# A fused 2-D Fourier transform and two-layer MLP on one core: x in six tiles of 128 partitions, the weights' sign decoded on ScalarE, four plain steps, and the order of all pieces written anew

## The chip, the core and the metric

One core of a Trainium2 chip runs the whole kernel. The metric is the device time of one execution in microseconds (us); three runs of the kernel before gave a median of 1582.02 us. Engines are named as in the profile: PE is TensorE's matmul, PEld its weight load, DVE is VectorE, ACT is ScalarE, POOL is GpSimd, SP is SyncE, which issues the DMAs.

## What is computed

```python
def reference(x, moe_w_in, moe_w_out, moe_s, moe_b):
    # x: 8 x 3008 x 256, float32
    X = np.fft.fft(x, axis=1)
    X = np.fft.fft(X, axis=2)
    t = X.real.astype(np.float32).reshape(8 * 3008, 256)
    h = t @ moe_w_in                       # 256 x 2048
    r = np.maximum(h, 0.0)
    g = moe_s * (r * r) + moe_b
    return (g @ moe_w_out).astype(np.float32)   # 2048 x 256
```

## The kernel before

The eight batches of x are called `su` = 0 to 7. For each, x is read in tiles of 96 partitions by 1024 numbers (`load`, eight tiles for a batch), folded by sums and differences into `cs`, and turned by small matmuls with tables `dft_sb` into the spectrum (`transform`, twice a batch: `ph` 0 and 1, four `pair` calls of eight small matmuls each). The Nyquist column is done apart for all batches at once (`nyquist`). The transform along the features is not made at all: it is folded into `w_in` by matmuls with a table `feat_sb` (`fold_w_in`, four pieces f = 0 to 3).

The weights arrive as words of 64 bits. `decode` turns one piece of 128 x 512 words into float32: two passes on ACT, two operations on DVE (one shifts, one puts the sign in) and one add on POOL. Sixteen pieces are decoded, eight of `w_in` and eight of `w_out`.

After that comes the long part: 8 batches x 3 blocks of 502 columns x 16 slices of the hidden layer are 384 steps. In a step `first_layer` (letter L) makes six matmuls of 502 columns, three per kind, from the spectrum's high and low part and `w_in`'s; DVE forms `even` and the two halves of `h`, ACT takes relu, square and a rounded copy `gh`, POOL or DVE the rest `gl`. `second_layer` (letter S) makes twelve matmuls of 502 columns. The first PLAIN steps are different: ACT takes relu and square alone, and the second layer has four float32 matmuls (eight records in the profile) straight from the decoded `w_out`, before that is split into a high and a low part.

Work is issued in the order of a list written by hand: `START` and, for each further batch, `BATCH` are strings of letters, and each letter runs the next piece of one generator (l: load a piece of the next batch's x, v and o: its transforms, L, G, S: first layer, the low part, second layer; X, x, y: load and fold batch 0; r, a, b, e: load and decode weights; w: fold a piece of `w_in`; n, m: Nyquist; s, u: the transforms of batch 0). `_in_order` then keeps each engine in that order. Six tiles of x, the raw words and several working tiles share buffers, so a load waits until the tile before it was read.

Of the kernel before, what the change touches and what calls it, by code (L numbers as in the profile page):

```python
# [15 lines left out]
P = 128  # L16
# [4 lines left out]
R = 96  # L21
# [6 lines left out]
ENGINES = tuple(getattr(mybir.EngineType, e) for e in ("PE", "DVE", "Activation", "Pool"))  # L28
# [11 lines left out]
Y_ON_VECTOR = (0, 1, 2, 5)  # L40
X_ON_VECTOR = (0, 1, 2, 3, 5, 6, 7)
LOADS_ON_GPSIMD = ()
SUMS_ON_SCALAR = ()
PLAIN = 6
WORDS = (
    ("in", 0, 0), ("in", 0, 1), ("in", 1, 0), ("in", 1, 1), ("out", 0), ("out", 1), ("in", 2, 0), ("out", 2),
    ("in", 2, 1), ("out", 3), ("in", 3, 0), ("out", 4), ("in", 3, 1), ("out", 5), ("out", 6), ("out", 7),
)
START = (
# [7 lines left out]
)  # L57
BATCH = (
# [60 lines left out]
def _dft_tables():  # L119
# [3 lines left out]
    out = np.zeros((R, 2, 2, 8, NL), np.float64)  # L123
# [84 lines left out]
def _lay_out_x(x):  # L208
# [8 lines left out]
    xq = np.ascontiguousarray(padded[:, rows[..., None], order[swap]])  # L217
    xn = np.ascontiguousarray(padded[:, rows, P].transpose(1, 2, 3, 0))
# [18 lines left out]
def kernel(ctx: ExitStack, tc: tile.TileContext, xq, xn, dft, turn, feat, w_in, w_out, s, b, out):  # L237
# [10 lines left out]
    act = ctx.enter_context(tc.tile_pool(name="act", bufs=3))  # L248
    outp = ctx.enter_context(tc.tile_pool(name="outp", bufs=2))
# [16 lines left out]
    turn_sb = const.tile([R, 8], F32, name="turn_sb")  # L266
# [4 lines left out]
    wo_h = const.tile([P, NJ, D], F32R, name="wo_h")  # L271
    wo_l = const.tile([P, NJ, D], F32R, name="wo_l")

    def words(part):
        if part[0] == "out":
            f = part[1]
            return w_out[f * 256:(f + 1) * 256].rearrange("(j p) (d t) -> p j (d t)", p=P, t=2)
        _, f, c = part
        return w_in[c * P:(c + 1) * P, None, f * 1024:(f + 1) * 1024]

    def load_words(part, pool, tag):
        raw = pool.tile([P, 512, 2], I32, name="raw", tag=tag)
        src = words(part)
        nc.sync.dma_start(raw.rearrange("p (j d) t -> p j (d t)", j=src.shape[1]), src)
        return raw

    halves = {}
    wny_dram = dram.tile([1, FF], F32, name="wny_dram")

    def decode(part, raw, aux):  # L290

        low, high = raw[:, :, 0], raw[:, :, 1]
        bits = aux if len(aux.shape) == 2 else aux[:, 1]
# [11 lines left out]
        if part[0] == "in":  # L305
            halves[part[1:]] = w, aux[:, 0].bitcast(F32)
        yield
# [15 lines left out]
    def fold_w_in(f):  # L323

        (w0, row), (w1, _) = (halves[f, c] for c in range(2))
        row = row[0:1]
        at = slice(f * 512, (f + 1) * 512)
        for kind in range(2):
            ps = bank()
            for c, w in enumerate((w0, w1)):  # L330
                nc.tensor.matmul(ps, feat_sb[:, c, kind * P:(kind + 1) * P], w, start=c == 0, stop=c == 1)  # L331
            if f == 0 and kind == 1:

                column = ps_o.tile([P, 512], F32, name="po")
                for i in range(4):
                    for c, w in enumerate((w0, w1)):
                        nc.tensor.matmul(  # L337
                            column[:, i:i + 1], w[:, i * P:(i + 1) * P], feat_sb[:, c, P:P + 1],
                            start=c == 0, stop=c == 1,
                        )  # L340
            yield
            if kind == 1:
                if f == 0:
                    nc.scalar.copy(wny[:, :4], column[:, :4])
                else:
                    nc.scalar.copy(row, ps[0:1])
            split(wd_h[:, kind, at], wd_l[:, kind, at], ps, nc.vector)
        if f > 0:
            nc.sync.dma_start(wny_dram[:, at], row)
            nc.sync.dma_start(wny[:, 4 * f:4 * f + 4], wny_dram[0, at].rearrange("(j p) -> p j", p=P))  # L350
# [53 lines left out]
    def nyquist(ph, t, room):  # L404
# [3 lines left out]
        cs = t[:, :, 2 * ph + 1]  # L408
# [55 lines left out]
        e = room if ph else outp.tile([P, 2 * NT], F32, name="e", tag="o")  # L464
# [419 lines left out]
```

## Time and profile before

| | us |
|---|---|
| runs | 1581.05, 1582.02, 1583.15 |
| median | 1582.02 |
| span of the profiled execution, first to last instruction | 1580.4 |
| PE busy / PEld / DVE / ACT / POOL | 1557.5 / 1372.7 / 1208.8 / 1227.1 / 912.5 |

Busy time is the time in which an engine has an instruction at work; a wait is put down to what ended it. The span is one execution, and it lies 1.6 us under the median of the runs; what lies outside it is not in the profile. In timeline and chain lines the first number is the start in us from the span's start, the second the length in us.

### The profile page before, as it was taken

Reading aid. Unit: us, or ns where it says so; the run is one execution under the profiler, and the core shown is the slowest. Engines: PE = TensorE matmul, PEld = TensorE weight load, DVE = VectorE, ACT = ScalarE, POOL = GpSimd, SP = SyncE. Lnnn points to the kernel's source line nnn. Section 1 sums busy time; section 2 is a strip of 40 time slices with the busy share of each in tenths; the row PEclk is TensorE's granted clock in tenths of the full one; section 3 lists DMA queues with packets and bytes.
Section 4 is the critical chain, followed back from the end, with each engine's and each line's share of the span. In section 5 each row is a group of like instructions: output and inputs, shape, how many; then the busy total and the mean of one; then the engine's idle time right before and its main releaser. Section 6 shows DMA issues by size and latency. Waiting matters only on the chain.

```text
span 1580.4 us, 21929 instructions
## 1 busy us (share of the span) xinstructions
PE 1557.5 (99%) x7502; PEld 1372.7 (87%) x7502; DVE 1208.8 (76%) x1997; ACT 1227.1 (78%) x1305; POOL 912.5 (58%) x552
## 2 busy tenths in 40 slices
PE   5999999999999999999999999999999999999998
PEld 3688888888888888888988889888888888888887
DVE  7888788887868778687787878778787777865563
ACT  3889778877787787697877877778787778787886
POOL 4646556655565555565655656555566555665554
PEclk9999999999999999999999999999999999999999
DMA  7311211111002110121000210112101110000000
GB/s 209 98 57 57 63 31 34 47 57 43 8 28 72 31 44 7 37 64 46 27 33 21 63 37 27 34 30 64 53 1 34 47 47 34 8 27 33 1 26 27
DMA packets 25572, 67.41 MB, mean 43 GB/s; under 512 B 4915, under 2 KB 10259, under 8 KB 25462
## 3 DMA queue, kind: packets, MB, share of 16 engines
q1 hardware_dynamic: 25462, 66.01, 13.4%
q8 instruction: 60, 0.98, 0.3%
q14 instruction: 50, 0.41, 0.1%
HBM read 41.27 MB, written 24.73 MB: 42 GB/s over the span
## 4 chain that ended last, share of the span: by engine, by line
PE 98%; DMA 1%; DVE 0%; ACT 0%; SPq 0%; issue 0%; ACTq 0%; DVEq 0%
PE po L696 61%; PE ab L642 31%; PE ab L566 4%; PE po L687 1%; PE ab L331 1%; DMA dft_sb<-in_dft 1%; DMA xt<-in_xq 0%; PE ab L462 0%; DVE o L713 0%; PE po L337 0%; SPq L731 0%; ACT g L665 0%; ACT h L652 0%; ACTq L872 0%; DVE even L647 0%
## 5 line engine op out<-in xcount | busy, mean ns | idle before, releaser
L677 POOL TENSOR_TENSOR gl<-h,gh 128x1004 fp32r<-128x1004 f32 x372 | 803.1, 2160 | 562.9 <-ACT gh L674 402.8
L652 ACT ACTIVATE h<-h 128x1004 f32<-128x1004 f32 x384 | 398.4, 1037 | 169.6 <-DVE h L651 168.4
L674 ACT CAST gh<-h 128x1004 fp32r<-128x1004 f32 x378 | 389.0, 1029 | 123.2 <-PE po L696 113.1
L647 DVE SCALAR_TENSOR_TENSOR even<-ebc,wny,ab 128x502 f32<-128x502 f32 x384 | 281.9, 734 | 239.5 <-PE ab L642 230.9
L696 PE MATMUL po<-gh,wo_h 128*128 128x502 f32 (+1 forms) x1512 | 445.9, 376 | 0.1
L696 PE MATMUL po<-gh,wo_l 128*128 128x502 f32 (+1 forms) x1512 | 443.5, 375 | 0.0
L668 ACT ACTIVATE h<-h 128x1004 f32<-128x1004 f32 x378 | 393.5, 1041 | 12.0
L696 PE MATMUL po<-gl,wo_h 128*128 128x502 f32 (+1 forms) x1512 | 381.8, 375 | 0.0
L696 PEld LDWEIGHTS po<-gl,wo_h 128*128 128x128 f32 x1512 | 285.8, 189 | 34.3
L696 PEld LDWEIGHTS po<-gh,wo_l 128*128 128x128 f32 x1512 | 285.6, 189 | 34.4
L696 PEld LDWEIGHTS po<-gh,wo_h 128*128 128x128 f32 x1512 | 282.8, 189 | 34.2 <-DVE o L713 0.4
L650 DVE TENSOR_TENSOR h<-even,ab 128x502 f32<-128x502 f32 x384 | 260.2, 678 | 66.9 <-POOL gl L677 17.1
L642 PE MATMUL ab<-spec_h,wd_h 128*128 128x502 f32 x768 | 292.3, 381 | 0.0
L642 PE MATMUL ab<-spec_l,wd_h 128*128 128x502 f32 x768 | 288.3, 375 | 0.0
L642 PE MATMUL ab<-spec_h,wd_l 128*128 128x502 f32 x768 | 287.1, 374 | 0.0
L651 DVE TENSOR_TENSOR h<-even,ab 128x502 f32<-128x502 f32 x384 | 257.7, 671 | 0.0
L642 PEld LDWEIGHTS ab<-spec_h,wd_h 128*128 128x128 f32 x768 | 144.6, 188 | 19.9 <-issue 1.0
L642 PEld LDWEIGHTS ab<-spec_l,wd_h 128*128 128x128 f32 x768 | 144.7, 188 | 18.1 <-issue 1.2
L642 PEld LDWEIGHTS ab<-spec_h,wd_l 128*128 128x128 f32 x768 | 145.0, 189 | 17.5
L713 DVE TENSOR_SCALAR o<-po,sb_s,bias 128x502 f32<-128x502 f32 x94 | 68.8, 794 | 37.3 <-PE po L696 37.3
L554 POOL TENSOR_TENSOR spec_l<-o,spec_h 128x368 fp32r<-128x368 f32 (+3 forms) x80 | 62.8, 805 | 50.0 <-ACT spec_h L552 49.3
L497 DVE TENSOR_TENSOR xt<-xt 96x512 f32<-96x512 f32 x56 | 56.4, 1007 | 0.0
(99 smaller groups left out, 707.0 us busy)
## 6 DMA issues: line engine op xcount, KB each, us to landing
xt<-in_xq SPq DMA_DIRECT2D x64, 384.0 KB
out<-o SPq DMA_DIRECT2D x46, 502.0 KB
raw<-in_w_in SPq DMA_DIRECT2D x8, 512.0 KB
raw<-in_w_out SPq DMA_DIRECT2D x8, 512.0 KB
ebc<-e_dram SPq DMA_DIRECT2D x16, 251.0 KB
ebc<-e_dram SPq DMA_DIRECT2D x8, 126.0 KB
out<-o SPq DMA_DIRECT2D x4, 251.0 KB
ebc<-e_dram SPq DMA_DIRECT2D x8, 125.0 KB
```

The source lines that it names most:

```text
L554: nc.gpsimd.tensor_sub(lo, src, hi.bitcast(F32))
L566: nc.tensor.matmul(ps[:, kind, i], src[:, i, kind * P:(kind + 1) * P], dft_sb[:, ph, kind, leaf + i], start=True, stop=True,)
L642: nc.tensor.matmul(beside(ps[kind]), w[:, kind, fj], in_turn(m[:, kind]), start=i == 0, stop=i == 2)
L647: nc.vector.scalar_tensor_tensor(beside(even), in_turn(ebc), wny[:, j:j + 1], beside(ps[0]), op0=ALU.mult, op1=ALU.add)
L650: sub(h[:, 1], even, ps[1])
L651: add(h[:, 0], even, ps[1])
L652: nc.scalar.activation(h, h, AF.Relu)
L668: nc.scalar.activation(h, h, AF.Square)
L674: nc.scalar.copy(gh_halves, h)
L677: engine.tensor_sub(gl_halves, h, gh_halves.bitcast(F32))
L696: nc.tensor.matmul(beside(po[2 * pm + dh][:, :n]), l[:, j, dh * P:(dh + 1) * P], in_turn(r[:, pm])[:, :n // 2], start=start and i in (0, 2 ...
L713: nc.vector.tensor_scalar(o[:, dh], po[2 * pm + dh][:, :NT], *args, ALU.mult, ALU.add)
```

## The change

- x comes in six tiles of 128 partitions instead of eight of 96. Leaves 2 to 7 keep partitions 0 to 95; leaves 0 and 1 are cut in three strips of 32 each, which ride in partitions 96 to 127 of the six tiles, and a copy on ACT (`gather`) carries each strip to its place. The tables `dft`, `turn` and the Nyquist rows are padded to 128 partitions.
- `decode` sets the sign on ACT: the first pass is now a Prelu with a slope, and DVE's second operation is gone.
- `fold_w_in` takes all four Nyquist rows of `w_in` by a row of the matmul and a trip through DRAM; the column of sixteen small matmuls for f = 0 is gone. It runs one half of the input at a time.
- Buffers of their own (`late`, `IN_SLOTS`) for raw words and decoded weights; x's first four tiles lie in the second `cs`.
- PLAIN is 4 instead of 6. `first_layer` is cut in two pieces (L: matmuls, D: the rest), the stores of batch 0 too; folding batch 0 is cut in rows, pairs and halves.
- `START` and `BATCH` are new, and SP is kept in order too.

```diff
-PLAIN = 6
+IN_SLOTS = ((0, "h"), (0, "h"), (0, "h"), (0, "gh"), (0, "gl"), (0, "gl"), (1, "xt"), (1, "xt"))
+NX = 6
+PLAIN = 4
 START = (
-    "X X n X X X r t x y X x r r x x X t x a X s a n t b y x b y x a s r x b e x c s s s r s n m a e s w b e w s e "
...
+    "X N r X a x n r d b x y c d y X X X g Y a b e k g X w x r s K t k t x d Y d x g g r e w t k y d k x y r a g K "
...
-    out = np.zeros((R, 2, 2, 8, NL), np.float64)
+    out = np.zeros((P, 2, 2, 8, NL), np.float64)
...
+    tile, part = np.arange(NX)[:, None], np.arange(P)[None, :]
+    leaf = np.where(part < R, tile + 2, tile // 3)
+    t = np.where(part < R, part, part - R + 32 * (tile % 3))
...
-        nc.scalar.activation(w, high.bitcast(F32), AF.Copy, scale=2.0 ** -112)
+        nc.scalar.activation(w, high.bitcast(F32), AF.Prelu, scale=2.0 ** -112, alpha=-(2.0 ** 32))
 
         nc.scalar.activation(low, low.bitcast(mybir.dt.uint32), AF.Copy, scale=2.0 ** -29)
         yield
 
-        nc.vector.tensor_scalar(bits, bits, 3, 0x7FFFFFFF, ALU.logical_shift_left, ALU.bitwise_and)
-        nc.vector.scalar_tensor_tensor(bits, high, -(1 << 31), bits, ALU.bitwise_and, ALU.bitwise_or)
+        nc.vector.tensor_scalar(bits, bits, 3, None, ALU.logical_shift_left)
...
+    def gather(cs, c, phases):
+
+        a, b_ = c // 3, c % 3
+        nc.scalar.copy(cs[32 * b_:32 * b_ + 32, phases, a], cs[R:, phases, c + 2])
+
     def load(su):
...
+        for c in range(NX):
+            t = stage.tile([P, 4, D], F32, name="xt")
+            nc.sync.dma_start(t, xq[su, c])
+            add(t[:, 0::2], t[:, 0::2], t[:, 1::2])
+            yield
+            add(t[:, 1], t[:, 0], t[:, 2])
+            yield
+            sub(t[:, 3], t[:, 0], t[:, 2])
+            yield
+            add(cs[:, :, c + 2, :P], t[:, 1::2, :P], t[:, 1::2, P:])
+            yield
+            sub(cs[:, :, c + 2, P:], t[:, 1::2, :P], t[:, 1::2, P:])
+            yield
+            gather(cs, c, slice(0, 2))
+            yield
...
-            if f == 0 and kind == 1:
-
-                column = ps_o.tile([P, 512], F32, name="po")
-                for i in range(4):
...
+        ps = [pool.tile([P, 512], F32, name=name) for _ in range(2)]
+        for c in range(2):
+            for kind in range(2):
+                nc.tensor.matmul(
+                    ps[kind], feat_sb[:, c, kind * P:(kind + 1) * P], halves[f, c], start=c == 0, stop=c == 1
+                )
+            yield
```

The new order on three engines, at the places that the prediction speaks of. SP, the first loads. Before (`room` holds the Nyquist rows, `xt` x, `raw` the weights' words):

```order
L722 DMA room<-in_xn 96x256
L723 DMA turn_sb<-in_turn 96x8
L731 DMA xt<-in_xq 96x1024 x5
L284 DMA raw<-in_w_in 128x1024
L743 DMA dft_sb<-in_dft 96x2x384
L731 DMA xt<-in_xq 96x1024
L284 DMA raw<-in_w_in 128x1024 x2
L731 DMA xt<-in_xq 96x1024
L743 DMA dft_sb<-in_dft 96x2x384
L731 DMA xt<-in_xq 96x1024
L743 DMA dft_sb<-in_dft 96x1536
L284 DMA raw<-in_w_in 128x1024
```

The same place now (x's first four tiles are called `cs`):

```order
L740 DMA cs<-in_xq 128x1024
L729 DMA room<-in_xn 128x256
L730 DMA turn_sb<-in_turn 128x8
L760 DMA raw<-in_w_in 128x1024
L740 DMA cs<-in_xq 128x1024
L760 DMA raw<-in_w_in 128x1024
L744 DMA feat_sb<-in_feat 128x2x256
L740 DMA cs<-in_xq 128x1024 x2
L740 DMA xt<-in_xq 128x1024 x2
L760 DMA raw<-in_w_in 128x1024
L752 DMA dft_sb<-in_dft 128x2x384 x2
L760 DMA raw<-in_w_in 128x1024
```

x's first tile goes first, two pieces of words and `feat_sb` come early, and the tables all stand behind the whole of x; the third piece of the tables is the next row.

PE, from the start. Before (L462 is Nyquist, L566 a transform's pair, L331 a fold of `w_in`, L337 its column):

```order
L462 MATMUL ab<-dft_sb,room 16x384
L462 MATMUL ab<-dft_sb,room 16x8x24 x2
L462 MATMUL ab<-dft_sb,room 16x2x48 x4
L462 MATMUL ab<-dft_sb,room 16x96 x2
L462 MATMUL ab<-dft_sb,room 16x192
L462 MATMUL ab<-dft_sb,room 16x96 x2
L566 MATMUL ab<-dft_sb,cs 128x96 x4
L566 MATMUL ab<-dft_sb,lf 128x96 x4
L331 MATMUL ab<-aux,feat_sb 128x512 x4
L337 MATMUL po<-feat_sb,aux 128x1 x8
L566 MATMUL ab<-dft_sb,lf 128x96 x4
L331 MATMUL ab<-cs,feat_sb 128x512 x4
```

Now (L325 is the fold, L449 Nyquist, L561 a pair):

```order
L325 MATMUL po<-bits,feat_sb 128x512 x4
L449 MATMUL ab<-dft_sb,room 16x384
L449 MATMUL ab<-dft_sb,room 16x8x24 x2
L449 MATMUL ab<-dft_sb,room 16x2x48 x4
L449 MATMUL ab<-dft_sb,room 16x96 x2
L449 MATMUL ab<-dft_sb,room 16x192
L449 MATMUL ab<-dft_sb,room 16x96 x2
L561 MATMUL ab<-dft_sb,cs 128x96 x4
L561 MATMUL ab<-dft_sb,lf 128x96 x4
L449 MATMUL ab<-dft_sb,room 16x384
L449 MATMUL ab<-dft_sb,room 16x8x24 x2
L449 MATMUL ab<-dft_sb,room 16x4x48
```

The fold of f = 0 has come to the front, the column is gone, and both Nyquist groups and the first two pairs follow without a fold between them.

DVE, up to the first step's `even` and `h`, now (`o_403` is the second half of batch 0's first spectrum, `wd_l` the low part of `w_in`'s piece f = 1):

```order
L569 TENSOR_TENSOR o_403<-x_168,t_399 128x4x96
L570 TENSOR_TENSOR o_403<-x_168,t_399 128x4x96
L298 TENSOR_SCALAR bits_333<-bits_333 128x512
L298 TENSOR_SCALAR whole_336<-whole_336 128x512
L569 TENSOR_TENSOR t_422<-ab_416,t_422 128x2x96
L570 TENSOR_TENSOR t_422<-ab_416,t_422 128x2x96
L569 TENSOR_TENSOR x_378<-t_395,t_422 128x8x48
L570 TENSOR_TENSOR x_378<-t_395,t_422 128x8x48
L263 TENSOR_TENSOR wd_l_96<-ab_413,wd_h_95 128x512
L263 TENSOR_TENSOR wd_l_96<-ab_412,wd_h_95 128x512
L647 SCALAR_TENSOR_TENSOR even_467<-ebc_355,wny_97,ab_450 128x502
L650 TENSOR_TENSOR h_468<-even_467,ab_451 128x502
```

In the kernel before, the rows between the same spectrum (`o_370` there) and `even` were three folds of x:

```order
L574 TENSOR_TENSOR o_370<-x_172,t_366 128x4x96
L575 TENSOR_TENSOR o_370<-x_172,t_366 128x4x96
L529 TENSOR_TENSOR xt_142<-xt_142 96x256
L530 TENSOR_TENSOR cs_104<-xt_142 96x128
L531 TENSOR_TENSOR cs_104<-xt_142 96x128
L647 SCALAR_TENSOR_TENSOR even_425<-ebc_346,wny_94,ab_417 128x502
L650 TENSOR_TENSOR h_426<-even_425,ab_418 128x502
```

What now stands there is the start of the second transform (`t_422`, `x_378`) and the low part of f = 1, which before was made ahead of the spectrum.

## Rows read from the trace of the kernel before

**Rows 1.** The page: span, and the chain that ended last, by engine.

```profile
span 1580.4 us, 21929 instructions
PE 98%; DMA 1%; DVE 0%; ACT 0%; SPq 0%; issue 0%; ACTq 0%; DVEq 0%
```

**Rows 2.** Waits of PE, 0 to 200 us: us in total, times, longest.

```profile
PE ab L462 <- DMA dft_sb<-in_dft: 17.1, 2, 14.3
PE po L687 <- ACT g L665: 0.4, 1, 0.4
```

**Rows 3.** Timeline of PE, 0 to 90 us: start, length, what, records.

```profile
14.35 4.00 PE L462 MATMUL ab<-dft_sb,room 96*16 96x384 f32 x14 [14.35 <-DMA dft_sb<-in_dft]
21.12 2.10 PE L462 MATMUL ab<-dft_sb,room 96*16 96x96 f32 x10 [2.77 <-DMA dft_sb<-in_dft]
...
26.82 6.29 PE L331 MATMUL ab<-aux,feat_sb 128*128 128x512 f32 x8
...
34.65 1.11 PE L566 MATMUL ab<-dft_sb,lf 96*128 96x96 f32 x8
35.60 3.62 PE L331 MATMUL ab<-cs,feat_sb 128*128 128x512 f32 x8
...
44.04 0.48 PE L642 MATMUL ab<-spec_h,wd_h 128*128 128x502 f32 x1
...
49.48 3.61 PE L687 MATMUL po<-g,whole 128*128 128x504 f32 x8 [0.36 <-ACT g L665]
...
59.05 1.03 PE L566 MATMUL ab<-dft_sb,lf 96*128 96x96 f32 x8
```

**Rows 4.** Busy time by stretch: PE, PEld, DVE, ACT, POOL; granted clock, DMA share, GB/s.

```profile
6.00:10.00 4.00, 0.00 (x0) 0.00 (x0) 3.86 (x11) 0.36 (x3) 0.00 (x0) 1.00 1.02 270
16.00:18.00 2.00, 2.00 (x12) 1.36 (x10) 2.00 (x3) 1.07 (x2) 1.92 (x4) 1.00 1.07 387
400.00:600.00 200.00, 200.00 (x981) 179.06 (x980) 156.50 (x258) 157.67 (x162) 117.71 (x62) 1.00 0.11 36
```

**Rows 5.** Timeline of all engines, 0 to 36 us.

```profile
5.70 0.69 DVE L514 TENSOR_TENSOR xt<-xt 96x512 f32<-96x512 f32 x1 [2.39 <-DMA xt<-in_xq]
...
7.62 0.68 DVE L514 TENSOR_TENSOR xt<-xt 96x512 f32<-96x512 f32 x1
...
9.08 0.68 DVE L514 TENSOR_TENSOR xt<-xt 96x512 f32<-96x512 f32 x1
...
15.76 1.34 POOL L304 TENSOR_TENSOR aux<-aux,raw 128x512 int32<-128x512 int32 x1 [1.48 <-issue]
15.99 1.26 DVE L530 TENSOR_TENSOR cs<-xt 96x128 f32<-96x128 f32 x1
...
26.76 0.35 DVE L574 TENSOR_TENSOR t<-ab,t 128x192 f32<-128x192 f32 x1
...
30.28 0.87 DVE L360 SCALAR_TENSOR_TENSOR lf<-uv,turn_sb 96x256 f32<-96x256 f32 x2
```

**Rows 6.** The chain that ended last, pieces from 40 to 62 and 139 to 148 us.

```profile
40.09 4.02 PE ab L462 x30
...
44.98 0.75 DVE even L647
...
55.84 3.37 PE po L687 x8
...
139.81 2.54 PE po L696 x12
...
147.44 1.27 PE ab L642 x6
```

**Rows 7.** Groups of instructions by shape: busy us and mean ns of one, idle before.

```profile
L652 ACT ACTIVATE h<-h 128x1004 f32<-128x1004 f32 x384 | 398.4, 1037 | 169.6 <-DVE h L651 168.4 <-POOL spec_l L554 1.1
L554 POOL TENSOR_TENSOR spec_l<-o,spec_h 128x380 fp32r<-128x380 f32 x8 | 8.4, 1049 | 20.4 <-ACT spec_h L552 20.4
L260 DVE TENSOR_TENSOR wd_l<-ab,wd_h 128x512 fp32r<-128x512 f32 x8 | 5.3, 684 | 1.6 <-ACT wd_h L259 1.6
```

More of the change, by code (lines that the diff above doesn't have):

```diff
@@ L323, in fold_w_in @@
     def fold_w_in(f):
-        (w0, row), (w1, _) = (halves[f, c] for c in range(2))
-        row = row[0:1]
         at = slice(f * 512, (f + 1) * 512)
[L328 to L331, printed above, removed]
-            if f == 0 and kind == 1:
-                column = ps_o.tile([P, 512], F32, name="po")
-                for i in range(4):
[L336 to L340, printed above, removed]
-            yield
[L342 to L350, printed above, removed]
-        yield
-    dft_sb = const.tile([R, 2, 2, 8, NL], F32, name="dft_sb")
+        pool, name = ((ps_ab, "ab"), (ps_o, "po"))[f in FOLDS_IN_SUMS]
+        ps = [pool.tile([P, 512], F32, name=name) for _ in range(2)]
[4 more added lines that the diff above has]
+                )
+            yield
+        row = rows[f][0:1]
+        nc.scalar.copy(row, ps[1][0:1])
+        split(wd_h[:, 1, at], wd_l[:, 1, at], ps[1], nc.vector)
+        yield
+        split(wd_h[:, 0, at], wd_l[:, 0, at], ps[0], nc.vector)
+        yield
+        nc.sync.dma_start(wny_dram[:, at], row)
+        yield
+        nc.sync.dma_start(wny[:, 4 * f:4 * f + 4], wny_dram[0, at].rearrange("(j p) -> p j", p=P))
+        yield
+    dft_sb = const.tile([P, 2, 2, 8, NL], F32, name="dft_sb")
     def stt(dst, a, col, other, engine=nc.vector):
-        factor = turn_sb[:, col:col + 1]
+        factor = turn_sb[:R, col:col + 1]
         if engine is nc.vector:
@@ L463, in nyquist @@
         yield
[L464 removed]
+        e = room if ph else act.tile([P, 2 * NT], F32, name="e", tag="gl")
         to = 0
@@ L524, in load_second, with load_rows @@
-    def load_second(tiles):
-        for c, t in enumerate(tiles):
-            v = folded[0][:R, 1, c]
-            engine = nc.vector if c in Y_ON_VECTOR else nc.gpsimd
-            engine.tensor_sub(t[:, 3], t[:, 0], t[:, 2])
-            engine.tensor_add(v[:, :P], t[:, 3, :P], t[:, 3, P:])
-            engine.tensor_sub(v[:, P:], t[:, 3, :P], t[:, 3, P:])
+            gather(cs, c, slice(0, 2))
+            yield
+    def load_rows(tiles):
+        for t in tiles_in_turn(tiles):
+            add(t[:, 0::2], t[:, 0::2], t[:, 1::2])
+            yield
@@ new lines, in load_pairs, with load_halves, tiles_in_turn @@
+    def load_pairs(tiles, ph):
+        for t in tiles_in_turn(tiles):
+            (sub if ph else add)(t[:, 1 + 2 * ph], t[:, 0], t[:, 2])
+            yield
+    def load_halves(tiles, ph):
+        for c, t in enumerate(tiles_in_turn(tiles)):
+            t, v = t[:, 1 + 2 * ph], folded[0][:, ph, c + 2]
+            add(v[:, :P], t[:, :P], t[:, P:])
+            sub(v[:, P:], t[:, :P], t[:, P:])
+            yield
+    def tiles_in_turn(tiles):
+        for i in range(NX):
+            yield tiles[i]
@@ L532, in load_second, with gathers @@
+    def gathers(ph):
+        for c in range(NX):
+            gather(folded[0], c, slice(ph, ph + 1))
             yield
@@ L621, in transform @@
             o = o.rearrange("p k r a g -> p k r (a g)")
-            store(su, ph, [(r, o[:, :, m]) for m, r in enumerate(range(4)[which])])
+            stores = store(su, ph, [(r, o[:, :, m]) for m, r in enumerate(range(4)[which])])
+            next(stores)
+            if su == 0:
+                yield
+            next(stores, None)
             yield
@@ L767, in go_on, with load_w_in, load_w_out @@
-    def go_on():
-        for i in range(len(WORDS)):
-            next(decoding[i])
+    def load_w_in():
+        for i in range(8):
+            f, c = i // 2, i % 2
+            pool, tag = IN_SLOTS[i]
+            raw = (stage if pool else act).tile([P, 512, 2], I32, name="raw", tag=tag)
+            nc.sync.dma_start(
+                raw.rearrange("p d t -> p (d t)"), w_in[c * P:(c + 1) * P, f * 1024:(f + 1) * 1024]
+            )
+            raws_in.append(raw)
+            yield
+    def load_w_out():
+        for f in range(8):
+            if f < 4:
+                raw = late.tile([P, 512, 2], I32, name="raw", tag=f"low{f}")
+            else:
+                raw = spare_quarter(f - 4).rearrange("p j d -> p (j d)").bitcast(I32)
+                raw = raw.rearrange("p (d t) -> p d t", t=2)
+            nc.sync.dma_start(
+                raw.rearrange("p (j d) t -> p j (d t)", j=2),
+                w_out[f * 256:(f + 1) * 256].rearrange("(j p) (d t) -> p j (d t)", p=P, t=2),
+            )
+            raws_out.append(raw)
+            yield
@@ new lines, with begin_w_in, begin_w_out @@
+    in_progress, out_progress = [], []
+    def begin_w_in():
+        for i in range(8):
+            bits = late.tile([P, 512], I32, name="bits", tag=f"high{i}")
+            f, c = i // 2, i % 2
+            halves[f, c] = bits.bitcast(F32)
+            if c == 1:
+                rows[f] = raws_in[i].rearrange("p d t -> p (d t)")[:, :512].bitcast(F32)
+            in_progress.append(decode(raws_in[i], bits))
+            next(in_progress[i])
+            yield
+    def begin_w_out():
+        for f in range(8):
+            out_progress.append(decode(raws_out[f], place(f).bitcast(I32)))
+            next(out_progress[f])
+            yield
@@ L770, in go_on @@
+    def go_on(progress):
+        for i in range(8):
+            next(progress[i])
             yield
@@ L824 @@
             first()
+        elif what == "D":
+            activate()
         elif what == "G":
-            next(lows.pop(0))
+            next(lows.pop(0), None)
         elif what == "S":
@@ L839 @@
                 first()
+            elif what == "D" and started:
+                activate()
             elif what == "G" and lows:
-                next(lows.pop(0))
+                next(lows.pop(0), None)
             elif what == "S" and pending:
```

160 lines of the change are left out of this document (65 added, 95 removed), and 23 rows, old and new, of tables (BATCH, START).

## The prediction

> **What bounds the kernel now.** I read the page first: the chain that ended last is PE for 98% of a span of 1580.4 us [rows 1]. Then PE's waits: in the first 200 us there are three, two of 17.1 us together on the tables `dft_sb` and one of 0.4 us [rows 2]; in the stretch of 400 to 600 us PE is busy all of the time, ACT 157.7 us and DVE 156.5 us of 200 [rows 4]. So from 49.5 us on PE's matmuls follow each other without a gap and the time is what they cost: 2.54 us for a second layer, 1.27 us for a first [rows 6]. The change leaves these twelve and six matmuls as they are. It can win only at the start, or in PE's own work, and it can lose anywhere by a new wait.
>
> The timeline of PE shows the start [rows 3]. The Nyquist group waits for the tables until 14.35 us and again until 21.12 us. After that PE works, but slowly: the eight records of the first fold take 6.29 us at 26.82 us, the same eight at 35.60 us take 3.62 us. The granted clock reads 1.00 in both, so I take the level from the records: half speed (1.2 GHz) until some 32 us, after short work with gaps, and full speed (2.4 GHz) after some 5 us of full-width matmuls. The first step's matmuls begin at 44.04 us, the first second-layer at 49.48 us.
>
> **PE's own work.** A plain second layer costs 3.37 us, a three-pass one 2.54 us [rows 6]; two plain steps fewer save 1.7 us. The column of sixteen records, which filled the time from the end of the fold to the pair at 34.65 us (some 1.6 us) [rows 3], falls away; it lies before the point from which I count below and so is in that difference already.
>
> **The loads.** From 6 to 10 us, with loads of 96 partitions, the queues moved 270 GB/s at a full share; from 16 to 18 us, with the words' 128 partitions, 387 GB/s [rows 4], which is 264 and 378 KiB per us. The bounds for the padded loads are these two; I take 378, since x and the tables now have the shape of the words. Data flows from about 2.3 us, and a load lands some 0.9 us after its turn, since its neighbours in the line run beside it. By this the old second table piece, with 4,899 KiB in the line up to its end, lands at 2.3 + 4899/264 + 0.9 = 21.8 us; measured 21.1 [rows 3]. In the new order x is all in after 4,484 KiB: 15.1 us. The table pieces end at 5,380, 5,764 and 7,044 KiB: 17.4, 18.4 and 21.8 us. At 264 KiB the last two would be 25.0 and 29.9 us.
>
> The Trainium skill ("SBUF — State Buffer", Door 1: The DMA port swizzle) speaks for the faster end: partitions 0 to 63 reach only half of the ports, all 128 reach all. An estimate from its asymptotes is 327 GB/s for 96 partitions against 436; the ratio 0.75 is near the rows' 0.70. By it the last table piece would land at 20 us instead of 21.8, which DVE's path below doesn't notice.
>
> **DVE to the first pair.** x's first tile was used at 5.70 us [rows 5], behind two small loads; now it is first in the line with 512 KiB, between 4.2 and 5.7 us, and I take 4.4. The first half of a tile's fold (four operations) takes from 7.62 to 9.08 us, 1.46 us, its first operation 0.68 of that [rows 5]; the other half is three of the small ones at 0.26, so a tile is 2.24 us and six are 13.4 us, of which the last 0.5 comes later. Before the first pair is taken up DVE also does seven smaller operations at about 0.4 us (Nyquist rows, three shifts of words, two sums) and two low parts of `w_in` at 0.684 us [rows 7]: 2.8 + 1.4. Waits for the second tile and the first words: 1 us. POOL's add of words stretches a DVE sum that runs beside it: 1.26 us at 15.99 us, under POOL's 1.34 us at 15.76 us, where such a sum is else some 0.26 [rows 5]. Two such adds fall here; between 0 and 2 us, I take 2. Together 4.4 + 12.9 + 4.2 + 1 + 2 = 24.5 us, against 26.76 us now [rows 5]; 22.5 without the stretch.
>
> PE meanwhile has the fold of f = 0 from about 9.6 us (words decoded on ACT, DVE, POOL, then `feat_sb`), at half speed to at most 16.4 us, then Nyquist when the tables come, and the first pair when the last strip is gathered, at 21 us. So far it is ahead of DVE.
>
> **From there to the first second-layer.** Today DVE goes from this point to the leaves in ten operations, 26.76 to 31.15 us [rows 5], 0.44 us each. The new order has one shift of words among them; nine operations bring the first two leaves, 24.5 + 3.9 = 28.4 us. PE's second Nyquist group (4.02 us at full speed [rows 6]) fits between 23 and 27.1 us, so the third pair starts at 28.4 and ends at 29.4. DVE's two sums into `o` wait for its own queue until 30.1: 31.0 us. Two casts on ACT (some 0.5 each): 32.0. Two low parts on POOL at 1.05 us [rows 7]: 34.1. The next `o` has the same buffer and waits for them; two sums, one of them beside a POOL add: 35.5. Then two shifts that overlap ACT's four short copies: 36.5; four operations for `t_422` and `x_378`: 38.3; `wd_l` twice: 39.7 us. That is where `even` of the first step starts. Behind these rows stands PE, whose step 0 needs `t_422`'s bank and whose fold of f = 2 needs both of `wd_l`'s; behind PE nobody is in a hurry. From `even` to the first second-layer it took 44.98 to 49.48, 4.5 us [rows 3, 6]. So it starts at 44.2 us, 5.3 us earlier.
>
> What PE has done by then differs: the fold of f = 2 (3.46 us by the step from 35.60 us to the next group) and one more pair (0.95 us, 34.65 to 35.60 [rows 3]) are done, one first layer (1.27) is not. That is 3.1 us more done. From here to the end of the plain steps PE has 22 us of work on my reckoning and waits 0.5 us once, for DVE's `wd_l` and `t` between steps 2 and 3; before it waits for nothing there.
>
> **The tight stretch behind.** From the fifth to the fourteenth step ACT has ten times three passes (relu, square, cast; 1.04 us for the first [rows 7], the others taken alike), 31 us, and some 12 us of words, casts and stores, 43 us; PE has ten steps of 3.81, a fold and a pair, 42.5 us. A tie: waits between 0 and 2 us, I take 0.8. After that a batch costs ACT 157.7 x 191/200 = 151 us of 191 plus six gathers of 32 x 512 numbers, which no row shows: between 0.3 (nothing is shorter than such a small copy) and 1.04 each (twice the columns [rows 7]), 2 to 6 us; hidden by 34 us of slack. DVE loses two tiles a batch. The Prelu I take like the copy that it replaces; if it were a third longer, it would be 0.2 us each, in ACT's idle time up to 30 us.
>
> **Sum.** 5.3 + 3.1 + 1.7 - 0.5 - 0.8 = 8.8 us. The profiled span would go to 1571.6 us. The median stands 1.6 us above its span, and I keep that: 1582.0 - 8.8 = 1573.2 us.
>
> **Rivals.** *PE falls back to half speed.* After the fold of f = 0 PE has nothing full-width until the fold of f = 1: a pause until the tables land, 1 to 4 us, then Nyquist and pairs. Today such work, from 21.12 us on, ran slow from its beginning to its end; at 34.65 to 44 us, where it stood between folds, it ran fast [rows 3]. If the clock falls in the pause, the first Nyquist group takes 6.1 us (4.00 + 2.10 [rows 3]) from 17.4 on, each pair 2, the second Nyquist group 8: the third pair ends at 37.5 instead of 29.4 us, all behind it moves by 8.1, the gain shrinks to 0.7 and the time is 1581.3. The Trainium skill ("TensorE: Matmul & The Clock Gate", The HAM clock gate) says that the array goes to half rate after idling and back when busy, which is this rival. Against it: the pause is short if the loads are fast.
>
> *Padding doesn't pay.* Loads still move 264 KiB/us: the third table piece lands at 29.9 us, the third pair ends at some 34.5, 5 us late: 1578.
>
> *Slower.* The new batch order makes PE wait in each of the seven later batches: ACT's `gather` stands in its queue until DVE has folded the tile, and the relu behind it, and with it PE's second layer, waits. To end slower than before by more than 3.2 us it takes 8.8 + 3.2 = 12 us, 1.7 us a batch. Against it: ACT and DVE each have over 30 us of slack in a batch, and PE holds up to five first layers ahead. At 2.5 us a batch it is 1573.2 + 17.5 = 1590.7.
>
> **How the numbers follow.** What a measurement of this kernel can tell from no change is about 0.2%, 3.2 us. Chances: the forecast 0.60, half speed 0.17, padding without effect 0.08, waits in the batches 0.15. Faster takes the first, 0.06 of the padding and 0.03 of the half-speed case, 0.69; the same are 0.02, 0.10 and 0.03, 0.15; slower are 0.04 and 0.12, 0.16. The forecast's own range: 2 us less on DVE's path without stretches, up to 2 more on ACT and 2 on slower loads, so 1569.5 to 1577. To leave out no more than two in ten I go to 1568.5 below and to 1583 above, which takes in the two rivals that end near 1578 and 1581.
>
> **What would show it.** Right: x's last tile lands by 16 us, `dft_sb`'s pieces by 22; the second fold starts at full speed; the first `even` near 40 us, the first plain second layer near 44; no wait of PE after 55 us. Wrong: Nyquist records twice as long as at 40.09 us; a wait of PE on ACT or DVE that comes back with every batch; waits of PE between 65 and 110 us that add up to more than 2 us.

## The result: 0.67% slower, and the profile after

The changed kernel takes 1592.04 us (median of 5 runs, 1591.39 to 1592.38) against 1581.46 us before (5 runs, 1580.04 to 1583.15): a ratio of 1.0067, interval 1.0056 to 1.0077. It is slower by 10.6 us where 8.8 us less were forecast. The span of the profiled execution is 1590.4 us.

The page of the changed kernel, its span and the chain that ended last by engine (compare [rows 1]):

```profile
span 1590.4 us, 21860 instructions
PE 94%; DVE 2%; ACT 0%; issue 0%; POOL 0%; ACTq 0%; DVEq 0%; POOLq 0%
```

PE's share of the chain fell by four points, so other engines now hold PE up. Waits of PE over the whole span (us in total, times, longest; [rows 2] before):

```profile
PE po L325 <- DMA feat_sb<-in_feat: 11.6, 1, 11.6
PE po L325 <- POOL bits L301: 8.2, 1, 8.2
PE ab L325 <- DVE wd_l L263: 2.2, 1, 2.2
...
PE po L696 <- POOL gl L676: 0.6, 1, 0.6
```

The waits for the tables `dft_sb` are gone, as meant. In their place PE stands 8.2 us behind POOL in the middle of its first fold. Timeline of PE in the changed kernel ([rows 3] before):

```profile
11.60 3.75 PE L325 MATMUL po<-bits,feat_sb 128*128 128x512 f32 x4 [11.60 <-DMA feat_sb<-in_feat]
23.55 3.78 PE L325 MATMUL po<-bits,feat_sb 128*128 128x512 f32 x4 [8.20 <-POOL bits L301]
27.26 4.27 PE L449 MATMUL ab<-dft_sb,room 96*16 96x384 f32 x24
31.46 1.13 PE L561 MATMUL ab<-dft_sb,cs 96*128 96x96 f32 x8
...
33.41 4.09 PE L449 MATMUL ab<-dft_sb,room 96*16 96x384 f32 x30
37.43 2.02 PE L561 MATMUL ab<-dft_sb,lf 96*128 96x96 f32 x16
...
50.50 3.47 PE L325 MATMUL ab<-bits,feat_sb 128*128 128x512 f32 x4 [2.15 <-DVE wd_l L263]
...
56.79 3.54 PE L686 MATMUL po<-g,whole 128*128 128x504 f32 x8
```

The first half of the fold is done by 15.4 us, the second begins at 23.55, and the Nyquist group and the first pair follow it directly. The first plain second layer starts at 56.79 us, against 49.48 before and 44.2 forecast. What POOL and DVE did meanwhile (timelines of both; the last two rows are from a later batch):

```profile
9.48 1.79 POOL L301 TENSOR_TENSOR bits<-bits,raw 128x512 int32<-128x512 int32 x1 [1.51 <-ACT raw L295]
10.04 1.51 DVE L509 TENSOR_TENSOR cs<-cs 128x256 f32<-128x256 f32 x1
...
13.50 10.00 POOL L301 TENSOR_TENSOR bits<-bits,raw 128x512 int32<-128x512 int32 x1 [2.23 <-ACT cs L479]
13.69 0.68 DVE L504 TENSOR_TENSOR cs<-cs 128x512 f32<-128x512 f32 x1
...
21.95 0.41 DVE L298 TENSOR_SCALAR bits<-bits 128x512 int32<-128x512 int32 x1
...
27.94 1.28 POOL L301 TENSOR_TENSOR bits<-bits,raw 128x512 int32<-128x512 int32 x1
...
32.98 0.36 DVE L569 TENSOR_TENSOR t<-ab,t 128x192 f32<-128x192 f32 x1 [2.44 <-ACT t L575]
...
576.31 2.14 POOL L676 TENSOR_TENSOR gl<-h,gh 128x1004 fp32r<-128x1004 f32 x1 [1.10 <-PE ab L641]
577.16 1.96 DVE L347 SCALAR_TENSOR_TENSOR lf<-cs,turn_sb 96x256 f32<-96x256 f32 x2
```

POOL's second add of words took 10.00 us; an add of the same size takes 1.28 us at 27.94. From 13.29 to 22.36 us DVE ran thirty folds, sums and shifts with no gap, and POOL ended 1.14 us after the last of them, 21.95 + 0.41 = 22.36. Not every meeting goes so: POOL's first add, at 9.48 us, also met a DVE that was busy without a gap, and it was done in 1.79 us while DVE's operation at 10.04 took 1.51 us instead of 0.41. At 577.16 us it is the other way round: two DVE operations that took 0.87 us in [rows 5] take 1.96, because POOL's `gl` was there first. The share of busy time by stretch (PE, PEld, DVE, ACT, POOL, granted clock, DMA share, GB/s; [rows 4]):

```profile
10.00:20.00 10.00, 3.75 (x4) 1.17 (x4) 10.00 (x30) 4.74 (x11) 7.77 (x2) 0.97 1.04 405
20.00:30.00 10.00, 6.45 (x14) 2.33 (x15) 3.85 (x13) 2.79 (x7) 8.44 (x23) 0.52 0.50 178
400.00:600.00 200.00, 199.99 (x980) 177.72 (x979) 165.65 (x249) 162.14 (x169) 116.11 (x61) 1.00 0.11 36
```

The padded loads do move 405 GB/s. DVE is full from 10 to 20 us and busy for 3.85 us of the next 10: from 22.36 to 28.51 us it waits for the fold that waits for POOL. In that second stretch the granted clock is 0.52 in the mean, PE mostly at 1.2 GHz.

### The profile page after: what moved, and what is told of

It reads as the page before. It is cut to its first block, busy times and chain, and to the rows that moved or that the text cites. A ratio compares the mean times of both kernels' runs of the same rounds, so it can differ in the third digit from the quotient of the medians.

```text
span 1590.4 us, 21860 instructions
## 1 busy us (share of the span) xinstructions
PE 1559.5 (98%) x7494; PEld 1367.2 (86%) x7494; DVE 1251.7 (79%) x1912; ACT 1268.6 (80%) x1361; POOL 916.6 (58%) x541
## 4 chain that ended last, share of the span: by engine, by line
PE 94%; DVE 2%; ACT 0%; issue 0%; POOL 0%; ACTq 0%; DVEq 0%; POOLq 0%
PE po L696 60%; PE ab L641 30%; PE ab L561 3%; PE po L686 1%; DVE uv L347 0%; DVE even L647 0%; DVE h L650 0%; DVE h L651 0%; PE ab L325 0%; DVE gl L676 0%; POOL gl L676 0%; DVE x L569 0%; ACT h L667 0%; ACT h L652 0%; DVE wd_l L263 0%
## 5 line engine op out<-in xcount | busy, mean ns | idle before, releaser
L561 PEld LDWEIGHTS ab<-dft_sb,lf 96*128 96x128 f32 x384 | 47.9, 191 | 4.3 <-DVE even L647 1.8
```

The costliest lines, as they stand in the source:

```text
L561: nc.tensor.matmul(ps[:, kind, i], src[:, i, kind * P:(kind + 1) * P], dft_sb[:R, ph, kind, leaf + i], start=True, stop=True,)
```

## The experiments

Theory at the start: POOL's add was shut out by DVE's gap-free train, and PE, not DVE, set the first pair. Rivals: the Prelu, the clock, the batches. Letters are those of `START` and `BATCH`; z (a wait or an extra operation on DVE) and h (unread matmuls) are new. Three dots in an edit stand for code that is left out here. Unless said otherwise, times are medians of 5 runs or more, and before, run beside them on the same chip, had medians of 1581.39 to 1582.06 us. Line numbers in later kernels are up to three higher.

**e1_wait.** DVE waits once for the add, in front of the train.

```diff
+    touched = const.tile([P, 1], F32, name="touched")
+    def door():
+        nc.vector.tensor_copy(touched, halves[0, 1][:, :1])
+        yield
...
-  ... Y a b e k g X w x r s K t k t x d Y d x g g r e w t k ...
+  ... Y a b e e z k g X w x r s K t k t x d Y d x g g r w t k ...
```

> The changed kernel, with one copy of a single number on DVE that reads the result of POOL's second add of words and so makes DVE wait for it once; nothing else. In the changed kernel that add takes 10.0 us (13.50 to 23.50) while DVE runs sums of two tiles without a gap. Theory (DVE's sums keep POOL out of a port that both need; POOL gets in when DVE pauses): the add takes 1.3 to 1.8 us, the second half of the first fold starts near 15.6 us instead of 23.55, the first pair's sum on DVE at 26 instead of 32.98 us, and the time falls by 4 to 8 us to 1584 to 1588. Rival 1 (the add is slow by itself, from its buffers or the loads beside it): it still takes about 10 us, now with DVE waiting for it, and the time rises to 1595 to 1602. Rival 2 (the late fold costs nothing that isn't waited for anyway; the loss comes from the later order): the add is short, but the time stays within 2 us of 1592.

1589.73 us, ratio 1.0044 (1.0031 to 1.0058): 2.3 us back. Timelines of POOL, DVE, ACT and PE in e1:

```profile
12.71 1.28 POOL L301 TENSOR_TENSOR bits<-bits,raw 128x512 int32<-128x512 int32 x1 [2.24 <-ACT cs L479]
14.02 0.15 DVE L807 COPY touched<-bits 128x1 f32<-128x1 f32 x1 [1.44 <-POOL bits L301]
15.20 8.03 POOL L349 TENSOR_TENSOR room<-room,turn_sb 96x8 f32<-96x8 f32 x1
23.10 1.27 DVE L263 TENSOR_TENSOR wd_l<-po,wd_h 128x512 fp32r<-128x512 f32 x2
27.79 0.84 ACT L404 ACTIVATE room<-room 96x64 f32<-96x64 f32 x5 [4.00 <-POOL room L350]
28.25 6.20 PE L449 MATMUL ab<-dft_sb,room 96*16 96x384 f32 x30 [2.90 <-ACT room L404]
28.54 0.29 ACT L575 COPY t<-ab 128x192 f32<-128x192 f32 x1
```

The add takes 1.28 us, and the lock-out moves one item down POOL's queue: one operation on 96 x 8 numbers, 0.20 us elsewhere, takes 8.03. It ends at 23.23 us, just as DVE comes to the first operation behind the train that reads PSUM (`wd_l<-po`, 23.10). Two small operations ahead of it, at 14.08 and 14.50 us beside the same train, took only 0.35 and 0.73 us. ACT's five copies wait for POOL's chain, and the copy of `t` stands behind them in ACT's queue: `t` at 28.87 us instead of 32.98, and 24.5 forecast.

**e2_door, e4_strided.** A DVE operation with one input in place of the wait, its 512 elements adjacent (e2) or 8 bytes apart (e4): does that let POOL in?

```diff
+        nc.vector.tensor_scalar(wd_l[:, 1, 1536:], halves[0, 0], 1.0, None, ALU.mult)                              # e2
...
+        nc.vector.tensor_scalar(wd_l[:, 1, 1024::2], raws_in[0][:, :, 1].bitcast(F32), 1.0, None, ALU.mult)  # e4
```

> The changed kernel, with one extra DVE operation of 128 x 512 numbers that has a single input, put into the middle of the row of sums about half a microsecond after POOL's second add could start; DVE waits for nothing. Theory (only sums of two tiles keep POOL out, one after the other): the add starts during the extra operation and ends near 15.5 us, the next sum on DVE stretches by about 1 us, and the time is that of the run with the wait within 2 us, 1584 to 1588. Rival 1 (slow by itself): the add still ends near 23.5 us and the time is 1592 or more. Rival 3 (any busy DVE keeps POOL out): the add still ends near 23.5 us, time 1592 to 1594.

> Changed kernel with both adds of the first words ahead of DVE's long train and, in the place where e2 had a contiguous operation with one input, a DVE operation with one input whose 512 elements lie 8 bytes apart (a scale of the words' high halves into a part of wd_l that is overwritten later; the result is untouched). Theory A, only DVE operations that run at two elements a beat or read two SBUF tiles keep POOL out: POOL's second add begins under the strided operation, is done by 16 us, the fold's second half starts by 17 us, DVE loses about 1 us, first plain second layer near 55 us, 1589 to 1590.5 us. Rival B, any DVE operation that follows the one before without a gap keeps POOL out: the add again takes 10 us and ends at 23 us, 1591.5 to 1592.5 us.

1592.31 and 1592.69 us: no. Timeline of e4:

```profile
14.55 10.33 POOL L301 TENSOR_TENSOR bits<-bits,raw 128x512 int32<-128x512 int32 x1 [2.23 <-ACT cs L479]
14.75 0.41 DVE L805 TENSOR_SCALAR wd_l<-raw 128x512 fp32r<-128x512 f32 x1
```

The strided operation took the same 0.41 us as the adjacent one, so e4 did not make a slower DVE operation and doesn't separate its two theories. What is shown: during one operation with a single SBUF input, at 0.41 us for 512 elements, POOL's add got in no more than between the sums; in e1 the operation with an operand in PSUM did not keep POOL out.

**e3_before_prelu.** The kernel before with the sign decoded on ACT.

```diff
-        nc.scalar.activation(w, high.bitcast(F32), AF.Copy, scale=2.0 ** -112)
+        nc.scalar.activation(w, high.bitcast(F32), AF.Prelu, scale=2.0 ** -112, alpha=-(2.0 ** 32))
```

> The kernel before, with the sign decoded on ScalarE alone (Prelu, and DVE's second operation of each piece gone), all else as before. Theory (PE waits there for the tables alone, so work taken from DVE is not on the path): no change, 1580 to 1583. Rival (DVE's decode holds up the chain to the first steps, or lets POOL's adds in): 2 to 6 us faster, 1576 to 1579. Rival (a Prelu is slower than a copy on ScalarE): its mean is over 0.8 us instead of 0.67 us, the time 1582 to 1585.

1581.24 us, ratio 0.9998 (0.9989 to 1.0007). The Prelu takes 0.68 us on ACT, as the copy before it did, and the time shows no difference.

**e5_nyquist_late, e6_late_alone.** The second Nyquist group off the path to `t`: ACT's five copies behind the copy of `t`, PE's group behind step 0's first layer. e5 has e1's wait, e6 hasn't.

```diff
...
+        yield
         for n, sign in enumerate((1.0, 1.0, -1.0, -1.0, 1.0)):
...
-  ... w R K m s Y s a r n s b K s a s K R m a A ... R w i m s e u ... R A L A w E w D L D w ...
+  ... w R K m s Y s m a r n s b K s a s K R a A ... R w i s e u ... R A L m A w E w D m L D w ...
```

> e1 with three things moved: ACT's five copies for the second Nyquist group go behind its copy of t, PE's second Nyquist group goes behind step 0's first layer (into a bank of the second layer's), its copies and stores behind that. Theory: in e1 what stood ahead of t was ACT's queue, the five copies waiting for POOL's twenty small operations which DVE's train kept out; without them t comes at about 26 us instead of 28.87, the third pair some 3 us and, since 6 us of PE work are gone from ahead of it, step 0's first layer 4 us earlier, the second Nyquist group (4.1 us) fills the wait for wd_l; first plain second layer at 49 to 52 us instead of 54.76, 1585 to 1587.5 us. Rival: the chain from t on is bound by DVE, ACT and POOL whatever PE does, and the moved group pushes the fold of f = 2: first plain second layer at 54 us, 1589 to 1590 us.

> The same move of the second Nyquist group as in e5, in the changed kernel without e1's wait. Theory: as long as POOL's add ends at 23.5 us, the fold's second half, the first Nyquist group and the pairs follow it on PE, so t stays at 32 to 33 us; what is won is at most the group's share behind the third pair: 1590 to 1592 us. Rival: the late place of the second group alone, not POOL's add, is what costs the time: 1586 to 1588 us.

1589.97 and 1594.55 us: e5 wins nothing over e1, where the rival's time came out; e6 loses 2.5 us against the changed kernel, outside both. Timelines of DVE and PE in e5:

```profile
25.78 0.34 DVE L570 TENSOR_TENSOR t<-ab,t 128x192 f32<-128x192 f32 x1
...
29.38 0.43 DVE L298 TENSOR_SCALAR bits<-bits 128x512 int32<-128x512 int32 x1 [2.99 <-ACT bits L293]
...
32.82 3.73 PE L562 MATMUL ab<-dft_sb,lf 96*128 96x96 f32 x16 [6.72 <-DVE lf L368]
```

`t` comes at 25.78 us, as expected, but ACT's next pass over the words now stands behind the five copies, DVE's shift of them behind that, and DVE's queue behind the shift. And without the Nyquist group PE idles 6.72 us and does the next two pairs in 3.73 us instead of 2.02 (the same in e6, after 4.33 us of idle time). The granted clock is 0.50 from 33 to 36 us in e5, 1.2 GHz, and 1.00 from 37 to 40 us in the changed kernel, 2.4 GHz: there the group had kept PE busy up to the pair.

**e7_rows_early.** e1, and the leaves of the second group on DVE before 8.1 us, where it waits for words.

```diff
...
+        engine = nc.vector if ph else nc.gpsimd
...
-        nc.gpsimd.tensor_copy(lf[:, :2], cs[:, :2])
-        leaves_x(ph, cs, lf[:, 2:4], nc.gpsimd)
+        engine.tensor_copy(lf[:, :2], cs[:, :2])
+        leaves_x(ph, cs, lf[:, 2:4], engine)
...
-  X N r X a x n r d b ...  k n w R K m s Y ...
+  X N r X a x n m r d b ...  k n w R K s Y ...
```

> e1, and the second Nyquist group's eleven leaf operations, which POOL did as twenty-one small ones inside DVE's train, are done by DVE itself before 8.1 us, where it waits for the words; ACT's five copies follow the first group's, before 11 us. PE's order is that of the changed kernel, so the second group follows the first two pairs without a wait. Theory: t comes at about 26 us (28.87 in e1, 32.98 in the changed kernel), the second group runs at full speed behind the pairs, third pair at about 30 us, first plain second layer at 50.5 to 52 us (54.76 in e1): 1585 to 1587.5 us. Rival: PE falls to half speed wherever it is by then, or POOL's adds hit DVE's sums as often, and the chain behind t gives back what t wins: 1588 to 1590 us.

1590.18 us (1585.54 to 1591.65). The profiled execution is the fastest, 1585.54 us at a mean granted clock of 0.999; the others had 0.993 to 0.996 and 1588.3 to 1591.7. Timelines of PE, POOL and DVE in it:

```profile
29.85 2.02 PE L563 MATMUL ab<-dft_sb,lf 96*128 96x96 f32 x16
...
40.36 1.61 POOL L301 TENSOR_TENSOR bits<-bits,raw 128x512 int32<-128x512 int32 x1
40.75 1.64 DVE L572 TENSOR_TENSOR x<-t 128x384 f32<-128x384 f32 x1
...
49.55 3.54 PE L688 MATMUL po<-g,whole 128*128 128x504 f32 x8
```

With `t` at 25.76 us the third pair starts at 29.85 us, against 28.4 forecast. What is left shows in the two middle rows, DVE's sum waiting under POOL's add (0.55 us where none meets it), and in the clock. Theory and rival both hold part of it.

**e9_batch.** The changed kernel, one letter of `BATCH` moved.

```diff
-  ... L G S D S L o G L D S D S L ...
+  ... L G S D S L G L D o S D S L ...
```

> The changed kernel, in its batch order alone one leaf step of the second half of a transform moved behind one step's even and h, so that DVE's two operations on two SBUF tiles (577.16 us, 1.96 us instead of 0.87 under POOL's gl) come after gl is done. Theory: these collisions are what makes each of the six later batches 190.78 us instead of 190.10: 0.3 to 0.7 us a batch back, 1588 to 1590.5 us. Rival: the loss of a batch has another cause (the order of PE's own work or the other collision at 587 us): 1591.5 to 1592.5 us.

1589.02 us (1588.70 to 1589.29): 3.0 us back. In the profile a batch takes 190.19 us instead of 190.78 (190.10 in the kernel before). The two DVE operations take 0.87 us again. PE's matmuls show no wait between 560 and 760 us in either kernel; what is gone there are waits of its weight loads, 0.4 us for `gl` and 0.3 for `even`. Timelines of POOL and DVE in e9:

```profile
575.69 2.14 POOL L676 TENSOR_TENSOR gl<-h,gh 128x1004 fp32r<-128x1004 f32 x1 [1.09 <-PE ab L641]
...
578.59 0.87 DVE L347 SCALAR_TENSOR_TENSOR lf<-cs,turn_sb 96x256 f32<-96x256 f32 x2
```

**e10_words, e11_filler.** e10 is e7 with e9's batch and three word adds moved out of DVE's sums; e11 adds seven matmuls that nobody reads.

```diff
-  ... m s e u s s b u u s b w u B u e s w w w e w r a R A L A w E w D L D w ...
+  ... m s e b e u s s u u s w u u s w w w b B w r a R A L A w e E w D L D w ...     # e10
...
+                nc.tensor.matmul(ps, feat_sb[:, 0, :P], halves[0, 0], start=True, stop=True)   # e11, 2 + 3 + 2
```

> e7 with e9's batch order, and three of POOL's adds of words moved out of DVE's sums between t and wd_l: one in front, two behind (their DVE shifts with them). In e7's profile these adds stretch o by 1.1 us and x by 1.5 us. Theory: wd_l ends some 2.5 us earlier than in e7 (43.5 us) and the first plain second layer starts at 47 us instead of 49.55; with e9's 3.0 us the time is 5 to 6 us under e7's: 1584 to 1586 us. Rival: PE's later start or clock takes the 2.5 us, only e9's part shows: 1587 to 1588 us.

> e10 with seven more full-width matmuls of PE into a bank that nobody reads (two behind the fold of f = 0, three behind the first Nyquist group, two behind step 0's first layer), each set laid where PE waits in e7; the result is untouched. Theory: the runs of e7 between 1585.5 and 1591.7 us differ in granted clock (0.999 to 0.993), so what is left over the profile's chain is PE's half speed after such waits; with the fillers the clock is 0.998 or more in nearly all runs and the time is 2 to 4 us under e10's, with less spread. Rival: the clock doesn't depend on these waits; the fillers cost nothing or up to 1 us, same time and spread as e10.

e10: 1582.40 us (12 runs, 1579.09 to 1585.83), ratio 1.0001 (0.9992 to 1.0009). Its runs line up by granted clock: 1579.1 us at 0.999 and 1.000, 1581.2 to 1583.3 at 0.997, 1585.8 at 0.994. e11: 1580.52 us (11 runs, 1579.32 to 1581.19), 0.9991 (0.9982 to 1.0000), all at 0.999 or 1.000. Busy time of the stretch from 25 to 35 us in e10, and behind it the same stretch in e11 (columns as above):

```profile
25.00:35.00 10.00, 10.00 (x55) 7.03 (x54) 6.65 (x18) 7.47 (x20) 1.85 (x2) 0.66 0.60 204
```

```profile
25.00:35.00 10.00, 9.96 (x74) 7.75 (x73) 9.82 (x22) 8.79 (x24) 3.39 (x4) 1.00 0.60 195
```

PE is busy all of it in both, but at a granted clock of 0.66 it gets through 55 records and at 1.00 through 74. The medians differ by 1.9 us. e10's own two runs at 0.999 and 1.000 are 1.4 us faster than e11's median, so an estimate is that the seven matmuls cost 1.4 us themselves and that the clock costs e10 3.3 us in the median. In e11 `t` comes at 26.35 us and the first plain second layer at 47.83.

**e12_no_wait.** e11 without the wait, every other instruction in its place.

```diff
-  ... Y a b e e z k g X ... x g g r w h t k ...
+  ... Y a b e k g X ... x g g r e w h t k ...
```

> e11 without the one small DVE operation that waits for POOL's second add; every other instruction and its place is the same on every engine. Theory: DVE's train then starts before POOL's add, the add again takes some 10 us (1.28 in e11) and ends behind the train, the fold's second half starts near 23.5 us instead of 13.6, t comes at 32 to 33 us instead of 26.35, the first plain second layer 5 to 7 us later than in e11's 47.83: 1585.5 to 1588 us. Rival: with the Nyquist rows early, the batches and the words in better places, the late add is hidden, or the 10 us in the changed kernel had another cause: 1580 to 1582 us.

1590.18 us (1589.60 to 1590.71): 9.7 us slower than e11, more than expected. Timelines of POOL, PE and DVE in e12 (the first row holds two adds of words, the one that the fold waits for, 10.00 us, and the next, 1.28; L816 are the unread matmuls):

```profile
14.01 11.24 POOL L301 TENSOR_TENSOR bits<-bits,raw 128x512 int32<-128x512 int32 x2 [2.23 <-ACT cs L481]
24.06 3.38 PE L325 MATMUL po<-bits,feat_sb 128*128 128x512 f32 x4 [8.22 <-POOL bits L301]
27.27 1.88 PE L816 MATMUL po<-bits,feat_sb 128*128 128x512 f32 x4
...
32.13 2.84 PE L816 MATMUL po<-bits,feat_sb 128*128 128x512 f32 x6
...
36.23 0.36 DVE L571 TENSOR_TENSOR t<-ab,t 128x192 f32<-128x192 f32 x1 [5.59 <-ACT t L577]
...
57.71 3.54 PE L688 MATMUL po<-g,whole 128*128 128x504 f32 x8
```

The fold's second half waits 8.22 us again, `t` and the first plain second layer come 9.9 us later than in e11, and the time follows. But this isn't the price of the late add alone. In e11 the first five unread matmuls end at 25.09 us, about when the last strip is gathered (24.77). In e12 PE runs from 24.06 us to the pair without a pause, and they stand on that path with 4.7 us. From the fold's second half to the first pair it is 10.75 us in e12 (24.06 to 34.81) and 7.91 in the changed kernel (23.55 to 31.46), where the clock was lower. So the late add by itself costs 5 to 7 us; this is an estimate, 9.9 less 4.7 and 9.9 less 2.8.

**e13_batch1.** e11, one leaf step of batch 1 moved behind one step's `even`.

```diff
-  ... D G S o o L G G S L D D ...
+  ... D G S o L G G S L D o D ...
```

> e11, and in the first batch's order alone one leaf step moved behind one step's even and h, as in e9, so that DVE's four operations on two SBUF tiles (3.61 us at 228.78 us under POOL's gl, 1.66 else) come after gl. Theory: even there comes 3.6 us earlier, PE's wait of 0.6 us for gl and 0.4 for h in that batch goes: 0.5 to 1 us under e11's time, 1579.5 to 1580 us. Rival: the next gl meets the moved operations, nothing is won: 1580.5 us.

1578.51 us (11 runs, 1577.66 to 1580.00), ratio 0.9983 (0.9974 to 0.9992): it beats both kernels, and by 2.0 us e11, more than expected. Between the two profiles batch 1 alone gains 1.55 us (26.97 instead of 28.52 us from one copy of `t` to the next, from about 225 us on). Waits of PE in e13, over the whole span:

```profile
PE po L325 <- DMA feat_sb<-in_feat: 12.1, 1, 12.1
PE ab L643 <- DVE t L572: 0.6, 1, 0.6
PE ab L643 <- DVE h L653: 0.5, 2, 0.3
PE ab L643 <- POOL spec_l L551: 0.3, 1, 0.3
PE ab L643 <- DVE wd_l L263: 0.2, 1, 0.2
```

POOL's `gl` is gone from the list; after the first fold begins, PE waits 1.6 us in all.

## Why the prediction was wrong

**The step that failed** is in "DVE to the first pair": "POOL's add of words stretches a DVE sum that runs beside it ... I take 2." I read [rows 5], where POOL came first and DVE waited for it, and made DVE pay. In the new order DVE was first, with thirty operations and no gap, and POOL paid, 10.00 us. DVE's own path was right: by 22.36 us it had done all before the first pair but the low parts of `w_in`, which need the fold, and half of one tile. "So far it is ahead of DVE" of PE was the false sentence: the fold of f = 0, forecast to end at 16.4 us, ended at 27.3, and the first pair waited for it. `t` came at 32.98 us instead of 24.5, 8.5 late. e1 shows the cause, since with DVE's wait the add takes 1.28 us. e12 against e11 shows 9.7 us for the wait, of which some 5 to 7 are the late add by itself.

The Trainium skill ("SBUF — State Buffer", Who interferes with whom) says that VectorE and GpSimd share one pair of ports under an exclusive lock, which a VectorE operation with two inputs in SBUF contends for with a GpSimd operation that reads SBUF, and that whoever issues first holds it for its whole instruction while the other blocks. The trace agrees that it is exclusive (1.96 us instead of 0.87 under `gl`). It differs on how long: POOL was held not for one DVE instruction but for a train of thirty, most of them issued after POOL's span begins. Here the measurement decides. It doesn't say that POOL always loses: the first add at 9.48 us got in behind one operation. What lets POOL in between two DVE operations no run separates.

**From `t` to the first second-layer** I had 19.7 us (24.5 to 44.2), the changed kernel took 23.8 (32.98 to 56.79). The third pair came 4.5 us after `t` (forecast 3.9), `o`'s first sums were as forecast. Then `o` and `x` waited under two of POOL's word adds, 2.2 us together (1.63 and 1.64 us instead of 0.55) where I had counted one meeting; and the fold of f = 2 took 3.47 us for four records that take 1.91 elsewhere, at a granted clock of 0.57 from 50 to 54 us. With the adds moved that fold takes 1.98 us in e10, and in e11, where the clock holds too, this way is 21.5 us.

**The loads** were right in rate, 405 GB/s in the stretch where I took 387 from [rows 4]. Words and `feat_sb` landed 2 us later than reckoned (the fold began at 11.60 us, not 9.6). This doesn't show on the path: in e1, where the whole fold runs from 11.07 us on, PE still waits 2.04 us behind it.

**Plain steps, Prelu, gathers.** Eight records of a plain second layer take 3.54 us (3.61 in [rows 3]), the Prelu takes as long as the copy (e3), and a gather of 32 x 512 numbers takes 0.62 us, inside my bounds. The 1.7 us for two plain steps fewer rest on [rows 6]; no run tests them alone.

**The rivals.** *Half speed* did happen (a granted clock of 0.52 between 20 and 30 us), but as a consequence: in the changed kernel, e5 and e6 it follows PE's waits. By itself it cost e10 some 3.3 us in the median. *Padding* paid. *Slower* had the right sign and the wrong mechanism, so its 1590.7 us lie near the result by luck: six batches lose 0.7 us each (190.78 us against 190.10), not 1.7 to 2.5, and not behind the gathers, but where DVE's leaf operations, which now fall later in a batch, meet POOL's `gl`; e9 takes back 0.6 of each. I put the batches at nothing because of their slack of busy time; the slack was there (165.65 of 200 us on DVE), and the loss came all the same.

**The sum.** The profiled span missed its forecast by 18.8 us (1590.4 against 1571.6). The late `t` is 8.5 of them, the way from there to the first second layer 4.1, the six batches 4.1; the other 2.1 stay open.

**Why e1 won only 2.3 us:** it brought `t` forward by 4.1 us, and three more stalls stood in a row behind the first, POOL's Nyquist rows, ACT's queue and the clock. Only with all of them gone (e11) does the wait show what it is worth.

**Still open:** the best kernel stays 5.3 us above my forecast. Its `t`, at 27.44 us, is 2.9 us later than I reckoned, 1.45 of it the wait itself; the rest is not explained here.

## What to carry to other kernels

Look for a long train of DVE operations without a gap, and ask what POOL has to do beside it and who waits for that: POOL can pay for the whole train, not for one operation. A short wait of DVE at the right place (1.4 us) was worth 9.7 us in e11 and 2.3 in e1: it pays in full only when nothing else in POOL's and ACT's queues stands in the same shadow, so follow the queue to its next item before counting the gain. When you take out one change to price it, check that what you added beside it doesn't move onto the path. Price a meeting of the two engines from both sides, and in a loop move the meeting rather than the work: one letter gave 3.0 us.

## What was not expected of the hardware

- One POOL operation on 96 x 8 numbers was held for 8.03 us, and a word add for 10.00 to 10.33 us, by a DVE train, while an earlier add in the same kernel got in behind one operation (1.79 us). In e1 a DVE operation with an operand in PSUM did not keep POOL out; one with a single SBUF input, adjacent or strided (0.41 us for 512 elements), didn't let it in.
- Taking a group of matmuls out of a gap made PE slower: after 4.33 to 6.72 us of idle time the next pairs took 3.73 us instead of 2.02. Seven matmuls without a use, laid in the gaps, made the kernel 1.9 us faster in the median and narrowed its runs from 6.7 to 1.9 us.
